# Moving another square of the softmax through DRAM in the attention stage, and queueing the loads behind its return

## The chip, the cores and the metric

The kernel runs on one core of a Trainium2 chip, as one launch. The metric is the device time of one execution in microseconds (us). TensorE is called PE here, VectorE DVE, ScalarE ACT, GpSimd POOL, and SyncE SP. SP computes nothing: it issues the DMAs of this kernel, nearly all of them, in one queue and in the order of the program. POOL issues the scattered row writes.

## The reference

Two layers follow each other. First comes attention with a mask from hashing: a query and a key meet only where the signs of six random projections agree. Then every token goes to the one expert (of 8) that a gate picks.

```python
q_bits = (np.einsum('bhsd,dk->bhsk', q, proj) > 0)      # B=4, H=8, S=768, D=64; proj is 64 x 6
q_bucket = np.sum(q_bits * powers, axis=-1)             # k_bucket likewise
mask = q_bucket[:, :, :, None] == k_bucket[:, :, None, :]
scores = np.where(mask, scale * np.matmul(q, k.transpose(0, 1, 3, 2)), -1000000000.0)
attn = np.exp(scores - np.max(scores, axis=-1, keepdims=True))
attn = attn / (np.sum(attn, axis=-1, keepdims=True) + 1e-09)
out = np.matmul(attn, v)
...
x = out.transpose(0, 2, 1, 3).reshape(B * S, H * D)     # 3072 tokens of 512
expert_idx = np.argmax(x @ w_gate, axis=1)
h = np.maximum(xe @ w1[e], 0.0); out[mask] = gate_w[mask, None] * (h @ w2[e])
```

## The kernel before, in words

**Tiling.** The 32 heads are worked on as 16 pairs, 0 to 15. A pair has two groups, g = 0 and 1, of 384 queries each. A group has six steps, n = 0 to 5, for three blocks of 128 queries (jj) and the two heads of the pair (hh), n = 2·jj + hh. So n = 0 is (jj 0, hh 0), and n = 1 is (jj 0, hh 1), the second step of the group. Each step handles a block of 128 queries by 768 keys. This is the stage that the change touches; it takes the first 480 us or so. The experts' stage behind it is not touched.

**One step.** For step i the program writes, in this order:

- "S", lines L232 and L233: the scores of step i + 2, four matmuls into the PSUM tile `s` (two buffers). The first of each two takes the high part of keys (`k1`), the second the low part together with the twelve rows of hash codes (`k2`, `q2`).
- DVE takes the row maximum of `s` (L235, `m`) and two tiny operations on it (L236, L237).
- ACT takes the exponential of step i + 1 from `s` to the SBUF tile `p`, with the row sums to `sums` (L247). This frees the buffer of `s`.
- "T", L272: six transposes of `p` on PE against the identity into two PSUM tiles `t`, which ACT copies to `pt` (L275, two copies).
- In steps 1, 3 and 5, "AV", L288: eight matmuls of the group before, `pt` with `v`, into `o`. In step 1 "X" follows (L316): three transposes of the result of the group before that one, which DVE multiplies by the reciprocal of the sums (`inv`) into `xr`.

**The moved block.** In one step of a group the six transposes are left out. There the exponential writes its result to `pd` in another order, and the block goes out to a DRAM buffer (`moved`, four DMAs, L257) and back to SBUF (`pq`, one DMA, L260), which moves its 32 by 32 squares to their places. DVE then transposes each square (L263, STREAM_TRANSPOSE) into `pt`. Before the change this is step 0 of 27 groups, all but the first and the last four. DVE works in three parts of 128x256, at the tops of steps 0, 2 and 4 of the next group.

**Loads and operands.** `load_head` (L147 `kr`, L148 `qr`, 384 KB each) is issued a pair ahead of use, `load_codes` (L126, eight DMAs of 192 KB) for two pairs at a time, `load_v` (L153) at step 0 of g = 1. From `qr` POOL makes `q1` (L162, L171), and two DMAs fill `q2` from it and from the codes (L167, L168, in `sent`). From `kr` DVE and POOL make `k1` and `k2` (L178, L179), and one DMA brings the codes' rows into `k2` (L182, named k<-cr). `half_codes` makes the codes (L135 to L137). The list `later` holds DMAs to be issued at the top of a coming step, `heavy` operand work that is popped in steps 1, 3 and 5. In steps 19 to 47 every fourth step issues a `prefill` (L114, xs<-zrow, 910 KB), which writes the rows of the experts' input buffer; that is from pair 1 to the end of pair 3.

**Order.** PE, DVE, ACT and SP run in the written order. POOL's order is chosen by the framework's scheduler when the program is built. A wait of SP holds everything queued behind it.

Of the kernel before, what the change touches and what calls it, by code (L numbers as in the profile page):

```python
# [13 lines left out]
ALU = mybir.AluOpType  # L14
# [4 lines left out]
P = 128  # L19
B, H, S, D = 4, 8, 768, 64  # L20
NB = S // P
NPAIR = H // 2
# [7 lines left out]
SQ = 32  # L30
# [22 lines left out]
def bf(ap):  # L53
    return ap.bitcast(F32)
# [3 lines left out]
def lsh_attention_moe_kernel(ctx, tc, qd, kd, q2d, k2d, v, pjbd, wg, w1, w2, ident_in, tri_in, cols_in, eoff_in, ids_in, out):  # L58
    nc = tc.nc
    V, A, G, PE, SY = nc.vector, nc.scalar, nc.gpsimd, nc.tensor, nc.sync  # L60
# [58 lines left out]
    def load_codes(qi, hf, ks=(0, 1)):  # L119
        if qi not in xqs:  # L120
            xqs[qi] = ({}, codep.tile([P, S], F32R, name="cr"))
        for k in ks:
            pr = 2 * qi + k
            for j, src in enumerate((qd, kd)):
                t = xqp.tile([P, 384], F32, name="xq")
                SY.dma_start(out=t, in_=src[2 * pr:2 * pr + 2].rearrange("h d s -> (h d) s")[:, hf * 384:hf * 384 + 384])  # L126
                xqs[qi][0][(hf, 2 * k + j)] = t
# [13 lines left out]
    operands = {}  # L141

    def load_head(pr, hh):
        h = 2 * pr + hh
        qr = rawp.tile([P, S], F32, name="qr")
        kr = rawp.tile([P, S], F32, name="kr")
        SY.dma_start(out=kr, in_=k2d[h])  # L147
        SY.dma_start(out=qr, in_=q2d[h])  # L148
        return [qr, kr]
# [6 lines left out]
    later = []  # L156

    def q_operands(pr, hh, i):
        qr = operands[pr][0][hh][0]
        q1 = opp.tile([P, S], F32R, name="q1")  # L160
        q2 = opp.tile([P, S], F32R, name="q2")
        G.tensor_copy(out=q1, in_=qr)  # L162
        cr, cbase = codes[pr]
        c0 = cbase + NCODE * hh

        def sent():
            SY.dma_start(out=bf(q2[0:D]), in_=bf(q1[0:D]))  # L167
            SY.dma_start(out=bf(q2[D:D + NCODE]), in_=bf(cr[c0:c0 + NCODE]))  # L168

        later.append((i + 2, sent))  # L170
        G.tensor_tensor(out=q1[D:P], in0=qr[D:P], in1=bf(q1[D:P]), op=ALU.subtract)  # L171
        operands[pr][0][hh] += [q1, q2]

# [66 lines left out]
    def expo(s, m, sums, idx, moves):  # L240
        if moves:
            p = pdp.tile([P, S], F32, name="pd")
            to, of = p.rearrange("p (a c i) -> p c a i", a=4, i=SQ), s[:, 0:S].rearrange("p (c a i) -> p c a i", a=4, i=SQ)
        else:
            p = pp.tile([P, S], F32, name="p")
            to, of = p, s[:, 0:S]
        A.activation(to, of, AF.Exp, bias=m[:, 2:3], scale=m[:, 1:2], accum_out=sums[:, idx:idx + 1])  # L247
        return p

    def move(p, pt):  # L250
        way = moved[next(writes) % 2]
        q = pdp.tile([P, 4, 6, SQ], F32, name="pq")
        to = way.rearrange("(a j) s k -> s j a k", a=4)

        def out():
            for x in range(4):
                SY.dma_start(out=to[x], in_=p[SQ * x:SQ * x + SQ].rearrange("j (a k) -> j a k", a=4))  # L257

        def back():
            SY.dma_start(out=q, in_=way.rearrange("p s (c i) -> p s c i", i=SQ))  # L260

        def turn(c):
            V.transpose(out=pt[:, c:c + 2, 0:P].rearrange("p c (s j) -> p c s j", j=SQ), in_=q[:, :, c:c + 2].rearrange("p s c i -> p c s i"))  # L263

        return out, back, turn

# [13 lines left out]
    ots = {}  # L280
    invs = {}
    late = []

    def av(pr, g, pts, kcs, o, qs=slice(0, 384), heads=(0, 1)):
        vt = operands[pr][1]
        for kc in kcs:
            for hh in heads:
                PE.matmul(out=o[hh * D:hh * D + D, qs], lhsT=vt[:, kc, hh * D:hh * D + D], rhs=pts[hh][:, kc, qs],  # L288
                          start=kc == 0, stop=kc == NB - 1)

    def av_evac(pr, g, sums, o, defer):
        b, pi = divmod(pr, NPAIR)
        ot = otp.tile([P, 384], F32, name="ot")
        if defer:
            late.append(lambda: A.copy(out=ot, in_=o[:, 0:384]))
        else:
            V.tensor_copy(out=ot, in_=o[:, 0:384])
        ots[(b, g, pi)] = ot
        if (b, g) not in invs:
            invs[(b, g)] = smp.tile([P, 3, H], F32, name="inv", bufs=4)  # L300
        inv = invs[(b, g)][:, :, 2 * pi:2 * pi + 2]
        V.tensor_scalar(out=sums, in0=sums, scalar1=1e-9, scalar2=None, op0=ALU.add)
        V.reciprocal(out=inv, in_=sums.rearrange("p (j h) -> p j h", h=2))

    def av_out(pr, g):
        b, pi = divmod(pr, NPAIR)
        ot = ots[(b, g, pi)]
        inv = invs[(b, g)][:, :, 2 * pi:2 * pi + 2]
        if (b, g) not in xrows:
            xrows[(b, g)] = xrp.tile([P, 3, NG, RSEG], F32, name="xr")  # L310
            b0 = b * NB + 3 * g
            V.tensor_copy(out=xrows[(b, g)][:, :, :, SEG].bitcast(I32), in_=ids[:, b0:b0 + 3])
        x = xrows[(b, g)]
        xp = ps_m.tile([P, 512], F32, name="misc")
        for jj in range(3):
            PE.transpose(out=xp[:, jj * P:jj * P + P], in_=ot[:, jj * P:jj * P + P], identity=ident)  # L316
        V.tensor_tensor(
            out=x[:, :, pi, 0:SEG].rearrange("p j (h d) -> p j h d", h=2),
            in0=xp[:, 0:384].rearrange("p (j h d) -> p j h d", j=3, h=2),
            in1=inv.unsqueeze(3).broadcast_to([P, 3, 2, D]),  # L320
            op=ALU.mult)
# [186 lines left out]
    NPR = B * NPAIR  # L508
# [27 lines left out]
    turns = []  # L536

    def group(pr, g):
        if (pr, g) not in grp:
            grp[(pr, g)] = ([ptp.tile([P, NB, 384], F32, name=f"pt{x}", bufs=2) for x in range(2)],  # L540
                            smp.tile([P, 6], F32, name="sums", bufs=4))
        return grp[(pr, g)]

    def run_expo(i):
        pr, g, jj, hh = steps[i]
        moves = jj == 0 and hh == 0 and 0 < 2 * pr + g < 2 * NPR - 4
        p = expo(*soft.pop(i), group(pr, g)[1], 2 * jj + hh, moves)
        if moves:
            out, back, turn = move(p, group(pr, g)[0][hh])
            later.extend([(i, out), (i + 2, back)])  # L550
            turns.extend((i + 6 + c, partial(turn, c)) for c in (0, 2, 4))
        else:
            probs[i] = p

# [16 lines left out]
    def pick_first():  # L571

        def most():
            keys()
            V.reduce_max(out=best[:, 0:1], in_=key, axis=AX.X)

        def which():
            V.tensor_scalar(out=mark[:, 0], in0=key, scalar1=best[:, 0:1], scalar2=None, op0=ALU.is_equal)
            V.tensor_tensor(out=mark[:, 1], in0=mark[:, 0], in1=eoff[:, 0], op=ALU.mult)
            V.reduce_sum(out=best[:, 1:2], in_=mark[:, 1], axis=AX.X)  # L580
            V.tensor_scalar(out=best_i, in0=best[:, 1:2], scalar1=-1.0, scalar2=float(E), op0=ALU.mult, op1=ALU.add)

        return [most, which]
# [115 lines left out]
    light = []  # L699

    def out_and_route(pr, g):
        if pr % NPAIR < NPAIR - 1:
            av_out(pr, g)
            return

        pieces = route(pr // NPAIR, g)
        pieces[0]()
        light.append(lambda: av_out(pr, g))
        light.extend(pieces[1:])
        if (pr, g) == (NPR - NPAIR - 1, 1):  # L710
            light.extend(pick_first())
# [6 lines left out]
    run_scores(1)  # L718
    first_codes = [first_k(1, G), first_q(1, 0)]
    run_expo(0)  # L720
    for f in first_codes:
        f()
    SY.dma_start(out=h0[0][:, 384:S], in_=q2d[0][:, 384:S])
    prev, due, extra = None, [], {}
    for i, (pr, g, jj, hh) in enumerate(steps):
        n = 2 * jj + hh
# [6 lines left out]
            operands[pr + 1][1] = load_v(pr + 1)  # L733
        if pr == 0 and i == 0:
            operands[1] = [[load_head(1, hh) for hh in range(2)], None]
        if g == 1 and n == 1 and pr + 2 < NPR:
            operands[pr + 2] = [[load_head(pr + 2, 0)], None]
        if g == 1 and n == 4 and pr + 2 < NPR:
            operands[pr + 2][0].append(load_head(pr + 2, 1))
        if pr + 4 < NPR and ((pr, g, n) == (1, 0, 0) or g == 1 and n == 2 and pr % 2 == 0 and pr):  # L740
            for x in range(2):
                load_codes((pr + 4) // 2, x)
        if g == 0 and n == 0 and pr + 1 < NPR:
            for x in range(2):
                fs = [partial(q_operands, pr + 1, x), partial(k_operands, pr + 1, x)]
# [27 lines left out]
        if i + 1 < len(steps):  # L773
            run_expo(i + 1)
        while late:
            late.pop(0)()
        pts, sums = group(pr, g)
# [363 lines left out]
    with tc.If(nc.values_load(spare[0:1, E:E + 1], min_val=0, max_val=max(most), skip_runtime_bounds_check_because=why) > 0):  # L1141
# [10 lines left out]
        for e in range(E):  # L1152
            rows_apart("xs", G.indirect_dma_start(out=xs, out_offset=bass.IndirectOffsetOnAxis(ap=row[:, e:e + 1], axis=0),
                                                  in_=pad.rearrange("p g w -> p (g w)"), in_offset=None))
# [62 lines left out]
```

## Time and profile before

| | us |
|---|---|
| three runs before | 765.5, 769.04, 768.43; median 768.43 |
| the profiled execution | 765.38, with a span of 763.5 on the core |
| granted TensorE clock, mean over the span | 0.991 |
| PE busy | 734.3 (96% of the span) |
| DVE, ACT, POOL busy | 531.4 (70%), 459.6 (60%), 334.0 (44%) |
| DMA | 134.23 MB, 176 GB/s over the span |

How to read it: the span starts with the first instruction of the core and ends with the last, and all positions below are microseconds from its start. PE's weight loads are a row of their own (PEld), since they run beside matmuls. Matmuls overlap, so the start of one to the start of the next says more than its duration. A bracket behind a row of the timeline is the idle time of the engine ahead of it, and what the profile takes for the end of that wait. A row with x6 holds six instructions.

### The profile page before, as it was taken

How to read it: one execution, taken by the hardware profiler on the slowest of the kernel's cores; microseconds unless marked ns; L12 is line 12 of the kernel's file. 1: busy time of each engine (PE TensorE's matmuls, PEld its weight loads, DVE VectorE, ACT ScalarE, POOL GpSimd, SP SyncE). 2: the span in 40 equal slices, each digit the busy share in tenths (PEclk: the TensorE clock that was granted, in tenths of full speed). 3: DMA queues.
4: the chain of work that ended last, by engine and by line, in shares of the span. 5: the costliest groups of instructions: out<-in, count | busy, mean ns of one | idle time of the engine just before them, and what ended most of it. 6: DMA issues, size and time to landing. Idle time of an engine off the chain costs nothing.

```text
span 763.5 us, 13596 instructions
## 1 busy us (share of the span) xinstructions
PE 734.3 (96%) x4557; PEld 572.5 (75%) x4557; DVE 531.4 (70%) x1259; ACT 459.6 (60%) x939; POOL 334.0 (44%) x284
## 2 busy tenths in 40 slices
PE   6988997899999999999999999999999999999997
PEld 3645664566666666666667766999999999999995
DVE  6856776588877888877888786765656574665751
ACT  6756776577787777787778885343334343353430
POOL 2743333334632435524343460303747466383572
PEclk9999999799999999999999999999999999999999
DMA  5867798575675485575466330466464646656531
GB/s 180 255 203 227 190 306 242 166 258 146 194 252 172 102 280 159 167 264 161 115 210 203 107 100 29 144 174 171 146 171 143 182 149 190 180 184 192 169 107 45
DMA packets 84047, 134.23 MB, mean 176 GB/s; under 512 B 10278, under 2 KB 52390, under 8 KB 83968
## 3 DMA queue, kind: packets, MB, share of 16 engines
q1 hardware_dynamic: 78976, 120.59, 54.0%
q0 software_dynamic: 4992, 12.69, 4.6%
q8 instruction: 38, 0.62, 0.4%
q14 instruction: 41, 0.34, 0.2%
HBM read 94.37 MB, written 30.98 MB: 164 GB/s over the span
## 4 chain that ended last, share of the span: by engine, by line
PE 47%; issue 21%; POOL 14%; DMA 8%; DVE 6%; SPq 2%; ACT 2%; POOLq 0%; DVEq 0%; ACTq 0%
PE o L288 14%; PE t L272 11%; POOL y L992 10%; PE s L232 9%; PE s L233 7%; DMA y<-yo,tags 3%; DVE m L235 2%; PE misc L316 2%; POOL yo L990 1%; DMA q<-cr 1%; ACT p L247 1%; PE misc L135 1%; DMA qr<-q2d 1%; DMA xr<-xs 1%; DMA xre<-xs 1%
## 5 line engine op out<-in xcount | busy, mean ns | idle before, releaser
L235 DVE TENSOR_REDUCE m<-s 128x1 f32<-128x768 f32 x192 | 181.8, 947 | 54.5 <-PE s L233 43.7
L247 ACT ACTIVATE p<-s,m 128x768 f32<-128x768 f32 x165 | 164.9, 1000 | 61.8 <-DVE m L237 56.0
L275 ACT COPY pt<-t 128x384 f32<-128x384 f32 x330 | 141.1, 481 | 44.5 <-PE t L272 44.4
L232 PE MATMUL s<-k,q 128*128 128x512 f32 (+1 forms) x384 | 149.0, 389 | 5.4 <-ACT p L247 4.8
L288 PE MATMUL o<-pt,vt 128*64 128x384 f32 (+1 forms) x816 | 147.3, 486 | 0.0
L233 PE MATMUL s<-k,q 76*128 76x512 f32 (+1 forms) x384 | 124.7, 345 | 13.3 <-POOL q L171 6.3
L272 PE MATMUL t<-ident,p 128*128 128x128 f32 x990 | 136.9, 274 | 0.0
L232 PEld LDWEIGHTS s<-k,q 128*128 128x128 f32 x384 | 73.5, 191 | 65.4 <-ACT pt L275 22.9
L992 POOL DMA_INDIRECT y<-yo,tags x89 | 104.3, 1172 | 25.2 <-issue 22.5
L272 PEld LDWEIGHTS t<-ident,p 128*128 128x128 f32 x990 | 113.8, 141 | 1.8 <-issue 0.6
L179 POOL TENSOR_TENSOR k<-kr,k 64x768 fp32r<-64x768 f32 x30 | 54.7, 1824 | 125.2 <-DVE k L178 58.8
L233 PEld LDWEIGHTS s<-k,q 76*128 76x128 f32 x384 | 74.0, 193 | 23.8 <-POOL q L171 10.6
L288 PEld LDWEIGHTS o<-pt,vt 128*64 128x64 f32 x816 | 49.6, 137 | 50.7 <-issue 47.8
L950 ACT ACTIVATE hh<-hps 128x352 fp32r<-128x352 f32 (+3 forms) x56 | 27.9, 499 | 97.1 <-PE hps L964 97.1
L657 DVE TENSOR_TENSOR wlo<-wraw,whi 128x1024 fp32r<-128x1024 f32 x60 | 73.7, 1229 | 16.8 <-ACT whi L652 16.8
L983 PE MATMUL hps<-hh,whi 128*128 128x448 f32 (+10 forms) x224 | 76.2, 340 | 0.0
L983 PE MATMUL hps<-hh,wlo 128*128 128x436 f32 (+6 forms) x224 | 76.1, 340 | 0.0
L983 PE MATMUL hps<-hl,whi 128*128 128x436 f32 (+6 forms) x224 | 76.1, 340 | 0.0
L964 PE MATMUL hps<-xh,whi 128*128 128x352 f32 (+3 forms) x224 | 75.0, 335 | 0.0
L964 PE MATMUL hps<-xh,wlo 128*128 128x428 f32 (+6 forms) x224 | 74.8, 334 | 0.0
L964 PE MATMUL hps<-xl,whi 128*128 128x428 f32 (+6 forms) x224 | 74.8, 334 | 0.0
L171 POOL TENSOR_TENSOR q<-qr,q 64x768 fp32r<-64x768 f32 x30 | 55.2, 1841 | 20.4 <-DMA xs<-xr,slot 13.5
(218 smaller groups left out, 1074.8 us busy)
## 6 DMA issues: line engine op xcount, KB each, us to landing
wraw<-w SPq DMA_DIRECT2D x64, 512.0 KB
kr<-k2d SPq DMA_DIRECT2D x32, 384.0 KB
qr<-q2d SPq DMA_DIRECT2D x31, 384.0 KB
moved<-pd SPq DMA_DIRECT2D x108, 96.0 KB
pq<-moved SPq DMA_DIRECT2D x27, 384.0 KB
xs<-zrow SPq DMA_DIRECT2D x8, 910.0 KB
vt<-v SPq DMA_DIRECT2D x16, 384.0 KB
xq<-qd SPq DMA_DIRECT2D x30, 192.0 KB
```

Source lines behind the costliest of these rows:

```text
L171: G.tensor_tensor(out=q1[D:P], in0=qr[D:P], in1=bf(q1[D:P]), op=ALU.subtract)
L232: PE.matmul(out=s[:, c0:c1], lhsT=q1[:, qs], rhs=k1[:, c0:c1], start=True, stop=False)
L233: PE.matmul(out=s[:, c0:c1], lhsT=q2[0:KM, qs], rhs=k2[0:KM, c0:c1], start=False, stop=True)
L235: V.reduce_max(out=m[:, 0:1], in_=s[:, 0:S], axis=AX.X)
L247: A.activation(to, of, AF.Exp, bias=m[:, 2:3], scale=m[:, 1:2], accum_out=sums[:, idx:idx + 1])
L272: PE.transpose(out=t[:, i * P:i * P + P], in_=p[:, kc * P:kc * P + P], identity=ident)
L275: A.copy(out=dst, in_=src)
L288: PE.matmul(out=o[hh * D:hh * D + D, qs], lhsT=vt[:, kc, hh * D:hh * D + D], rhs=pts[hh][:, kc, qs], start=kc == 0, stop=kc == NB - 1)
L657: loeng.tensor_tensor(out=lo[:, i:i + step], in0=cell["t"], in1=bf(hi[:, i:i + step]), op=ALU.subtract)
L964: PE.matmul(out=hps[:, 0:w], lhsT=wt[:, c, fs], rhs=xt[:, c, 0:w], start=n == 0, stop=n == 3 * NDC - 1)
L983: PE.matmul(out=yps[:, 0:w], lhsT=wt[:, f, ds], rhs=ht[:, 0:w], start=n == 0, stop=n == 3 * NFC - 1)
L992: rows_apart("out", G.indirect_dma_start(out=out_seg, out_offset=bass.IndirectOffsetOnAxis(ap=tags[:, i, 0:1].bitcast(I32), axis=0), in_=y ...
```

## The change

It consists of these parts:

- The moved block is that of step 1 of a group (hh = 1), and only in the pairs 4 to 13, which makes 20 groups instead of 27. It goes out at the top of its step and its return is issued two steps later, as before. DVE turns its squares in one operation of 128x768 five steps later, at the top of step 0 of the next group.
- `load_head` of both heads moves from steps 1 and 4 of g = 1 to steps 3 and 4. `load_codes` moves from step 2 of g = 1 of an even pair, where all eight DMAs stood together, to steps 3 and 4 of g = 0, four in each. In the program they then stand behind the return of a block.
- The two DMAs of `sent` are issued one step after the operation instead of two for pair 1.
- The addition of 1e-9 to the sums goes from DVE to POOL for 29 of the groups, and DVE's reciprocal of them is held back until `out_and_route`, two steps later.

```diff
-        later.append((i + 2, sent))
+        later.append((i + (1 if pr == 1 else 2), sent))
...
-        def turn(c):
-            V.transpose(out=pt[:, c:c + 2, 0:P].rearrange("p c (s j) -> p c s j", j=SQ), in_=q[:, :, c:c + 2].rearrange("p s c i -> p c s i"))
+        def turn():
+            V.transpose(out=pt[:, :, 0:P].rearrange("p c (s j) -> p c s j", j=SQ), in_=q.rearrange("p s c i -> p c s i"))
...
-        V.tensor_scalar(out=sums, in0=sums, scalar1=1e-9, scalar2=None, op0=ALU.add)
-        V.reciprocal(out=inv, in_=sums.rearrange("p (j h) -> p j h", h=2))
+        if defer:
+            G.tensor_scalar(out=sums, in0=sums, scalar1=1e-9, scalar2=None, op0=ALU.add)
+            divide.append(lambda: V.reciprocal(out=inv, in_=sums.rearrange("p (j h) -> p j h", h=2)))
+        else:
+            V.tensor_scalar(out=sums, in0=sums, scalar1=1e-9, scalar2=None, op0=ALU.add)
+            V.reciprocal(out=inv, in_=sums.rearrange("p (j h) -> p j h", h=2))
...
-        moves = jj == 0 and hh == 0 and 0 < 2 * pr + g < 2 * NPR - 4
+        moves = jj == 0 and hh == 1 and NPAIR <= pr < NPR - 2
...
-            turns.extend((i + 6 + c, partial(turn, c)) for c in (0, 2, 4))
+            turns.append((i + 5, turn))
...
     def out_and_route(pr, g):
+        while divide:
+            divide.pop(0)()
...
-        if g == 1 and n == 1 and pr + 2 < NPR:
-            operands[pr + 2] = [[load_head(pr + 2, 0)], None]
-        if g == 1 and n == 4 and pr + 2 < NPR:
-            operands[pr + 2][0].append(load_head(pr + 2, 1))
-        if pr + 4 < NPR and ((pr, g, n) == (1, 0, 0) or g == 1 and n == 2 and pr % 2 == 0 and pr):
+        if g == 1 and n in (3, 4) and pr + 2 < NPR:
+            if n == 3:
+                operands[pr + 2] = [[], None]
+            operands[pr + 2][0].append(load_head(pr + 2, n - 3))
+        if (pr, g, n) == (1, 0, 0):
             for x in range(2):
-                load_codes((pr + 4) // 2, x)
+                load_codes(2, x)
+        if pr and pr % 2 == 0 and g == 0 and n in (3, 4) and pr + 4 < NPR:
+            load_codes((pr + 4) // 2, n - 3)
```

On SP, group 1 of pair 3, from its vt load to the first block of pair 4. Numbers at a name tell buffers apart; k<-cr brings key codes. Before:

```order
L153 DMA vt<-v 128x768
L167 DMA q_1485<-q_1484 64x768
L168 DMA q_1485<-cr 12x768
L147 DMA kr<-k2d 128x768
L148 DMA qr<-q2d 128x768
L114 DMA xs<-zrow 112x8x260
L260 DMA pq<-moved_61 128x768
L182 DMA k_1546<-cr 12x768
L147 DMA kr<-k2d 128x768
L148 DMA qr<-q2d 128x768
L114 DMA xs<-zrow 112x8x260
L257 DMA moved_62<-pd 32x4x192 x4
```

The same place now:

```order
L153 DMA vt<-v 128x768
L167 DMA q_1492<-q_1491 64x768
L168 DMA q_1492<-cr 12x768
L114 DMA xs<-zrow 112x8x260
L182 DMA k_1555<-cr 12x768
L147 DMA kr<-k2d 128x768
L148 DMA qr<-q2d 128x768
L147 DMA kr<-k2d 128x768
L148 DMA qr<-q2d 128x768
L114 DMA xs<-zrow 112x8x260
L257 DMA moved_61<-pd 32x4x192 x4
```

The loads of kr and qr and the return of a block, which stood ahead of the key codes, now stand behind them or are gone; the prefill still stands ahead.

On PE, steps 0 and 1 of group 1 of pair 6, from the scores of step 2 on. Before:

```order
L232 MATMUL s<-k_2195,q_2136 128x256
L233 MATMUL s<-k_2196,q_2137 128x256
L232 MATMUL s<-k_2336,q_2274 128x512
L233 MATMUL s<-k_2337,q_2275 128x512
L232 MATMUL s<-k_2336,q_2274 128x256
L233 MATMUL s<-k_2337,q_2275 128x256
L272 MATMUL t<-ident,p 128x128 x6
L288 MATMUL o<-pt_2438,vt 64x384
L288 MATMUL o<-pt_2439,vt 64x384
```

The same place now:

```order
L232 MATMUL s<-k_2199,q_2141 128x256
L233 MATMUL s<-k_2200,q_2142 128x256
L272 MATMUL t<-ident,p 128x128 x6
L232 MATMUL s<-k_2335,q_2275 128x512
L233 MATMUL s<-k_2336,q_2276 128x512
L232 MATMUL s<-k_2335,q_2275 128x256
L233 MATMUL s<-k_2336,q_2276 128x256
L289 MATMUL o<-pt_2439,vt 64x384
L289 MATMUL o<-pt_2440,vt 64x384
```

The six transposes have gone from between the second scores and AV to between the two scores.

On DVE, the end of group 0 and the start of group 1 of pair 6. Before:

```order
L237 TENSOR_SCALAR m<-m 128x1
L302 TENSOR_SCALAR sums<-sums 128x6
L303 RECIPROCAL inv<-sums 128x3x2
L178 CAST k_2628<-kr 128x768
L263 STREAM_TRANSPOSE pt_2438<-pq 128x2x128
L235 TENSOR_REDUCE m<-s 128x1
```

The same place now:

```order
L237 TENSOR_SCALAR m<-m 128x1
L178 CAST k_2642<-kr 128x768
L263 STREAM_TRANSPOSE pt_2440<-pq 128x6x128
L235 TENSOR_REDUCE m<-s 128x1
L236 TENSOR_SCALAR m<-m 128x1
```

The addition to the sums and the reciprocal have left this place, and the turn is the whole block instead of a third of it.

More of the change, by code (lines that the diff above doesn't have):

```diff
@@ L282, in lsh_attention_moe_kernel @@
     late = []
+    divide = []
     def av(pr, g, pts, kcs, o, qs=slice(0, 384), heads=(0, 1)):
```

## The prediction

> **What bounds the kernel now.** I began with the head of the page.
>
> ```profile
> span 763.5 us, 13596 instructions
> PE 734.3 (96%) x4557; PEld 572.5 (75%) x4557; DVE 531.4 (70%) x1259; ACT 459.6 (60%) x939; POOL 334.0 (44%) x284
> ```
>
> PE is the bound, idle for 763.5 − 734.3 = 29 us in all. PE's waits from 30 to 145 us say where it stands still:
>
> ```profile
> PE s L233 <- POOL q L171: 6.3, 1, 6.3
> PE s L233 <- DMA q<-cr: 3.7, 1, 3.7
> PE s L233 <- issue: 2.9, 1, 2.9
> ```
>
> They are single waits, all at the scores of step 1 of a group 0 (pairs 1, 2 and 4). They stand in these stretches, each one step long, with a step of the same work in pair 14 as the fourth row and a step 0 without AV as the fifth (length; PE, PEld, DVE, ACT, POOL busy; granted clock; DMA share; GB/s):
>
> ```profile
> 37.87:47.20 9.33, 5.63 (x29) 2.59 (x27) 2.93 (x8) 4.31 (x9) 6.13 (x5) 0.82 0.86 267
> 71.72:77.82 6.10, 3.21 (x22) 1.76 (x20) 2.84 (x8) 3.19 (x7) 4.22 (x5) 1.00 1.06 356
> 129.02:140.95 11.93, 5.64 (x21) 2.94 (x19) 3.41 (x9) 3.84 (x8) 6.04 (x5) 0.60 0.96 318
> 415.08:418.06 2.98, 2.98 (x22) 1.78 (x20) 2.80 (x9) 2.61 (x7) 0.44 (x1) 1.00 0.98 385
> 418.06:419.45 1.39, 1.39 (x12) 1.29 (x11) 0.40 (x2) 1.39 (x5) 0.00 (x0) 1.00 0.24 54
> 46.42 0.85 PE L135 MATMUL misc<-xq,pj 128*32 128x384 f32 x8
> ```
>
> The first stretch also holds code matmuls (the last row, 46.42 to 47.20, 0.78). The losses are 9.33 − 2.98 − 0.78 = 5.6, 6.10 − 2.98 = 3.1 and 11.93 − 2.98 = 8.9 us: **17.6 us** together. The waits are only 12.9 of them; the rest is the clock, 0.82 and 0.60 there. The timeline of the third:
>
> ```profile
> 125.05 0.46 SPq L147 DMA_DIRECT2D kr<-k2d  x1
> 125.56 0.43 SPq L148 DMA_DIRECT2D qr<-q2d  x1
> 126.04 0.42 SPq L114 DMA_DIRECT2D xs<-zrow  x1
> 126.58 0.49 SPq L260 DMA_DIRECT2D pq<-moved  x1
> 127.11 1.53 SPq L182 DMA_DIRECT2D k<-cr  x1
> 133.61 1.80 POOL L171 TENSOR_TENSOR q<-qr,q 64x768 fp32r<-64x768 f32 x1
> 135.79 0.76 PE L233 MATMUL s<-k,q 76*128 76x512 f32 x1 [6.29 <-POOL q L171]
> ```
>
> The waiting matmul needs the key codes (k<-cr, 36 KB), and they were queued behind 768 KB of heads, 910 KB of prefill and 384 KB of a returning block. The POOL operation named is for the next pair and isn't an operand. In the second stretch the profile names no releaser, in the first a code DMA. I take the code DMA for all three.
>
> **Stalls: what the change removes.** Seven blocks of the pairs 0 to 3 no longer travel (384 KB each way), and heads stand behind the codes. On SP the codes then follow only small copies and, for the second and third stall, one prefill. SP also no longer waits there for a block's landing before its return. For the first stall, `sent` of pair 1 is a step earlier and ahead of the heads. What remains: 910 KB at the 318 GB/s of the third stretch is 2.9 us. A bound for issue to use of a DMA is in these rows, a block's return and its first use, without a wait:
>
> ```profile
> 197.25 3.28 SPq L257 DMA_DIRECT2D moved<-pd  x4
> 202.13 0.34 SPq L260 DMA_DIRECT2D pq<-moved  x1
> 206.55 0.44 DVE L263 STREAM_TRANSPOSE pt<-pq 128x256 f32<-128x256 f32 x1
> ```
>
> That is at most 4.4 us. So codes issued behind a prefill are there after 7.3 us at worst. They are issued for step 2 and read by the scores issued at step 5, 5.8 us later if SP went no faster than PE (steps 2, 3 and 4: 1.39 + 2.98 + 1.39). But nothing in that stretch of SP's queue waits for PE except the load of v, so SP runs ahead. I take the whole gain, **−17.6**; its lower bound is two remainders of 7.3 − 5.8 = 1.5 us, −14.6.
>
> The Trainium skill ("TensorE: Matmul & The Clock Gate", section on the HAM clock gate) says the array falls to half rate after an idle window of about 3.4 us. By that rule remainders of 1.5 us would cost no clock; the trace agrees, since the waits of 6.3 and 3.7 us lowered the clock and that of 2.9 us (granted 1.00) did not.
>
> **Unmoved groups.** Two whole groups, one with a moved block (pair 6, g = 1) and one without (pair 14, g = 0):
>
> ```profile
> 206.69:219.74 13.05, 13.02 (x84) 8.90 (x82) 10.30 (x26) 10.53 (x25) 4.76 (x4) 1.00 0.63 193
> 413.69:427.09 13.40, 13.40 (x90) 9.50 (x88) 10.61 (x30) 11.37 (x27) 5.30 (x4) 1.00 0.45 155
> ```
>
> A moved block saves only 13.40 − 13.05 = 0.35 us today. The seven groups that no longer move pay it back: 7 × 0.35 = 2.5 at least, and where step 0 had saved more (0.81 us long instead of 1.01, as in the first two rows below; so in two of the seven), up to 1.39 − 0.81 = 0.58 each. I take **+3.0**. Their 14 more copies on ACT lie beside PE (ACT 11.37 of 13.40).
>
> **Moved groups.** Why is the saving small? Six transposes cost PE 0.69 us (their weight loads, third row). Before, step 0 without them runs into a full pair of score buffers: the next scores start 212.07 − 211.06 = 1.01 us on, though an unmoved step 0 takes 1.39 with 0.69 of it transposes.
>
> ```profile
> 169.94 0.50 PE L232 MATMUL s<-k,q 128*128 128x512 f32 x1
> 170.75 0.40 PE L232 MATMUL s<-k,q 128*128 128x512 f32 x1
> 203.02 0.69 PEld L272 LDWEIGHTS t<-ident,p 128*128 128x128 f32 x6
> 211.06 0.51 PE L232 MATMUL s<-k,q 128*128 128x512 f32 x1
> 212.07 0.50 PE L232 MATMUL s<-k,q 128*128 128x512 f32 x1
> 213.63 1.51 PE L288 MATMUL o<-pt,vt 128*64 128x384 f32 x8
> 215.38 0.48 PE L232 MATMUL s<-k,q 128*128 128x512 f32 x1
> 213.66 0.99 ACT L247 ACTIVATE p<-s,m 128x768 f32<-128x768 f32 x1 [1.27 <-DVE m L237]
> ```
>
> In step 1, AV and X follow the scores, 215.38 − 213.63 = 1.75 us of work that needs no buffer of `s`. Step 0 then takes 1.39 and step 1 (215.38 − 212.07 = 3.31) falls to 2.62, so the next scores come at 211.06 + 1.39 + 2.62 = 215.07. The exponential that frees their buffer ended at 214.65. So the 0.69 are saved whole: 13.40 − 0.69 = 12.71 per group, 0.34 less than now, × 20 = 6.8. In four of the groups step 0 took 0.81, as in the first two rows, so 0.1 is left there (0.4); for five with routing work beside step 0 I halve it (0.85); eleven gain all (3.7): **−5.0**, between 0 (PE waits for the exponential after all) and −6.8.
>
> **DVE, POOL, SP beside it.** The operations on `sums` (duration least/median/most, ns), then step 0 of pair 6, g = 1, two shapes of a transpose, and two sums of waits:
>
> ```profile
> L302 DVE TENSOR_SCALAR sums<-sums x31: 160/161/1116, 44.2 to 468.9; 128x6 f32<-128x6 f32 x31
> L420 POOL TENSOR_SCALAR sums<-sums x3: 210/216/233, 460.4 to 476.6; 128x2 f32<-128x2 f32 x3
> 210.45 0.16 DVE L302 TENSOR_SCALAR sums<-sums 128x6 f32<-128x6 f32 x1
> 210.64 0.19 DVE L303 RECIPROCAL inv<-sums 128x6 f32<-128x6 f32 x1
> 212.15 0.96 DVE L235 TENSOR_REDUCE m<-s 128x1 f32<-128x768 f32 x1 [0.51 <-PE s L233]
> L598 DVE STREAM_TRANSPOSE xt<-xr 128x448 f32<-128x448 f32 x8 | 4.6, 611 | 0.0
> L598 DVE STREAM_TRANSPOSE xt<-xrl 128x160 f32<-128x160 f32 x4 | 1.3, 335 | 1.8 <-DMA xrl<-xs 1.8
> POOL q L162 <- DMA qr<-q2d: 28.2, 8, 7.6
> DVE pt L263 <- DMA pq<-moved: 2.8, 2, 1.6
> ```
>
> From 160 to 448 elements a transpose grows by 276 ns, so 768 take about 611 + 320 × 0.958 = 0.92 us, against 0.44 for the part that stood there. The two operations on the sums go from this place (0.3), and DVE idled 0.51 us here, so the turn adds nothing to the maximum that follows. If that cover were gone, the cost would be at most 0.48 per group. AV, which reads the turned block, starts after about 2.1 us, the turn ends near 1.2. POOL gains 29 small additions; its nearest row is 128x2 at 216 ns, and POOL is 44% busy. The reciprocal waits for one two steps later (1.39 + 2.98 = 4.4 us), longer than two of POOL's operations of 1.80 (L171). If POOL stood in a wait for qr just then, DVE would wait with it, up to 7.6 − 4.4 = 3.2 us; that belongs to the first rival.
>
> The Trainium skill ("SBUF — State Buffer", section on the two sides of SBUF) speaks against this: VectorE and GpSimd share a port pair that one holds alone for a whole instruction. At 216 ns each, 29 more holds are 6.3 us, on the sum 0, because DVE has slack in every group; the trace has the lock's mark, L302 which lasts 0.16 us in most cases and 1.1 at worst.
>
> **The sum.** 765.38 − 17.6 + 3.0 − 5.0 = 745.8, against the profiled execution (span 763.5 and 1.9 around it). The median shown is 3.05 higher than that execution. I expect less spread without stalls and add 1.2, a part of it: **747**.
>
> **Rivals.**
> 1. *A wait for DMA stays in the early pairs* (prefill ahead of codes, or a load of heads now too late for POOL's cast, which already waited up to 7.6 us for qr). Half of the 17.6 remains: 747 + 8.8 = 756. For it: 910 KB still stand ahead, DMA share near 1. Against it: 7 × 768 KB less traffic there.
> 2. *Step 1 saves nothing*, because the exponential (0.4 us early by the sum above) comes late with the longer turn. Then a moved group takes 13.05 as now: 747 + 5.0 = 752.
> 3. *Slower: the return comes too late for the turn.* The block leaves one step later and is turned at the same step 0, three steps after its return's issue instead of four. In the order now: out 1.0 us after the scores of step 0, return 4.9 later (202.13 − 197.25), landed at most 4.4 later, so at 10.3, turn at 12.6: 2.3 us to spare. Each us beyond holds DVE, then AV, in 20 groups; the gain of 19.6 in the sum is gone at 0.98 us of mean wait. With 1.5 us: 746 + 30 = 776. For it: DVE already waited for a return twice, 2.8 us in all. Against it: loads now stand behind the return, and the DMA share in these groups is 0.63.
> 4. *No change that can be told*: stalls come back at other places of the early pairs, costing all 17.6, and the moved groups gain as much as the unmoved ones lose: 765.
>
> **How the numbers follow.** The forecast 0.68, rival 1 0.14, rival 2 0.10, rival 3 0.04, rival 4 0.04. The range takes rivals 1 and 2 in above (756) and below the whole −6.8, +2.5 and some relief for the first groups, which I put at 2 to 3 us: 741. Within 0.5% (3.8 us), about what a measurement of this kernel can tell from no change, lies rival 4; beyond it on the slow side rival 3. So faster 0.92, same 0.04, slower 0.04.
>
> **What would show it.** PE's waits at L233 in the pairs 1, 2 and 4 gone, clock 1.00 throughout those groups; group lengths near 12.7 us in the pairs 6 and 7 and 13.4 in the unmoved ones; step 0 at 1.39 and step 1 at 2.62; L263 twenty times at 0.92 us, with no wait for pq. A wait of DVE for pq, or of the reciprocal for POOL, would make it wrong.

## The result, and the profile after

The changed kernel takes 744.31 us (median of 4 runs, 743.5 to 745.42), and the kernel before took 767.97 beside it on the same chip (4 runs). The ratio is 0.9697, with a 95% interval of 0.967 to 0.9724: faster by 3%. The forecast was 747, with a range of 741 to 756. The profiled execution took 744.31 itself, with a span of 742.4. Some numbers of lines shift by a few: AV is L289 now, the sums are added on POOL at L304 and the reciprocal is L305. All ratios leave out the slow executions: one of 1426.59 us in experiment 2, one of 766.42 in experiment 5 and one of 785.68 of the kernel before, beside the experiments 10 to 12.

The head of the page after:

```profile
span 742.4 us, 13583 instructions
PE 728.5 (98%) x4599; PEld 575.5 (78%) x4599; DVE 516.6 (70%) x1169; ACT 466.2 (63%) x953; POOL 341.3 (46%) x313
```

PE is idle for 13.9 us instead of 29. Its waits in the attention stage (from 12 to 450 us) are almost gone; the three of 6.3, 3.7 and 2.9 us have become one of 0.5:

```profile
PE s L232 <- ACT p L247: 1.9, 4, 0.7
PE s L233 <- DMA k<-cr: 0.5, 1, 0.5
```

Where the 765.38 − 744.31 = 21.1 us went is seen from three stretches that begin and end at the same instructions: the groups 0 to 8 (numbered over all pairs, so that 8 is g = 0 of pair 4), the groups 9 to 27, and the rest. Columns are length; PE, PEld, DVE, ACT, POOL busy; granted clock; DMA share; GB/s. Before:

```profile
6.81:150.82 144.01, 127.58 (x762) 82.20 (x763) 99.57 (x239) 97.70 (x210) 56.39 (x40) 0.95 0.76 226
150.82:413.69 262.87, 260.92 (x1696) 174.46 (x1695) 216.00 (x599) 203.45 (x449) 111.84 (x82) 1.00 0.63 188
413.69:763.50 349.81, 343.39 (x2097) 315.41 (x2095) 212.87 (x418) 155.76 (x279) 164.56 (x157) 1.00 0.49 146
```

After:

```profile
7.22:135.46 128.24, 126.05 (x805) 85.20 (x805) 90.81 (x210) 102.59 (x223) 58.24 (x48) 1.00 0.69 208
135.46:392.36 256.90, 256.90 (x1696) 174.34 (x1694) 210.50 (x543) 204.99 (x449) 116.73 (x101) 1.00 0.65 192
392.36:742.40 350.04, 342.86 (x2097) 315.52 (x2095) 212.03 (x411) 155.64 (x278) 165.17 (x159) 1.00 0.50 147
```

The early groups gave 15.8 us, although PE has 43 more matmul records there; the groups 9 to 27 gave 6.0 with the same number of matmuls. In them PE is now busy without a gap (256.90 of 256.90). The rest (the last four groups and the experts' stage) is as it was, and the start is 0.4 later.

The three stretches that held the stalls, then a group with a moved block (pair 10, g = 0) and one without (pair 14, g = 0), after:

```profile
37.89:42.42 4.53, 3.99 (x29) 1.92 (x28) 2.34 (x6) 3.85 (x9) 2.20 (x3) 1.00 0.88 305
67.80:70.79 2.99, 2.99 (x21) 1.77 (x19) 2.33 (x6) 2.60 (x7) 2.89 (x3) 1.00 0.89 275
122.94:125.94 3.00, 3.00 (x22) 1.79 (x20) 2.33 (x6) 2.61 (x7) 2.91 (x3) 1.00 0.93 321
285.75:298.50 12.75, 12.75 (x85) 8.89 (x81) 10.55 (x23) 10.62 (x24) 8.70 (x8) 1.00 0.78 237
392.36:405.76 13.40, 13.40 (x89) 9.51 (x87) 10.35 (x25) 11.32 (x26) 5.54 (x5) 1.00 0.54 179
```

The steps of 9.33, 6.10 and 11.93 us are 4.53, 2.99 and 3.00, all at a granted clock of 1.00. An undisturbed first one would be 2.98 + 0.78 = 3.76, so 0.77 us are left there, and nothing in the other two. The 0.5 us wait in it ends at 38.91, 0.14 after the key codes land (38.77); SP's issue just ahead of theirs, `sent`'s q<-cr, took 1.99 us in this execution. SP at the third of these places, after:

```profile
113.72 0.50 SPq L114 DMA_DIRECT2D xs<-zrow  x1
114.27 0.74 SPq L182 DMA_DIRECT2D k<-cr  x1
119.74 0.33 SPq L147 DMA_DIRECT2D kr<-k2d  x1
```

The scores that read these codes (L233) start at 123.26 without a wait (the timeline of PE), 9.0 us after the issue. By its semaphore events in the trace the DMA landed at 120.30, after 6.0 us; that of pair 2 took 6.6. Before, PE went on 8.7 us after the issue (127.11 to 135.79), and the same events settle what it waited for in all three places: the key codes landed at 74.99 and 135.70 and PE went on at 75.08 and 135.79; at the first place the queries' codes of `sent` (q<-cr) landed at 41.91 and PE went on at 42.05.

Steps 0 and 1 of group 0 of pair 10, on PE, DVE and ACT, after (three pieces of the timeline):

```profile
290.13 0.50 PE L232 MATMUL s<-k,q 128*128 128x512 f32 x1
291.52 0.48 PE L232 MATMUL s<-k,q 128*128 128x512 f32 x1
292.39 1.51 PE L289 MATMUL o<-pt,vt 128*64 128x384 f32 x8
294.14 0.48 PE L232 MATMUL s<-k,q 128*128 128x512 f32 x1
...
289.52 0.97 DVE L263 STREAM_TRANSPOSE pt<-pq 128x768 f32<-128x768 f32 x1
291.22 0.96 DVE L235 TENSOR_REDUCE m<-s 128x1 f32<-128x768 f32 x1 [0.73 <-ACT pd L247]
...
292.71 0.99 ACT L247 ACTIVATE p<-s,m 128x768 f32<-128x768 f32 x1 [0.37 <-DVE m L237]
```

Step 0 takes 1.39, step 1 2.62. The exponential that frees the buffer ends at 293.70, 0.44 before it is needed. The turn ends 1.9 before AV reads it, and the maximum behind it waits for ACT, not for the turn. The groups of the new operations (busy, mean ns | idle before):

```profile
L263 DVE STREAM_TRANSPOSE pt<-pq 128x768 f32<-128x768 f32 x20 | 19.4, 969 | 0.0
L304 POOL TENSOR_SCALAR sums<-sums 128x6 f32<-128x6 f32 x29 | 6.9, 237 | 39.4 <-ACT p L247 30.3 <-DMA pq<-moved 7.6
L305 DVE RECIPROCAL inv<-sums 128x6 f32<-128x6 f32 x29 | 5.2, 181 | 0.0
```

DVE waited for a returned block in no group, and for POOL's sums in none.

### The profile page after: what moved, and what is told of

It reads as the page before. It is cut to its first block, busy times and chain, and to the rows that moved or that the text cites. A ratio compares the mean times of both kernels' runs of the same rounds, so it can differ in the third digit from the quotient of the medians.

```text
span 742.4 us, 13583 instructions
## 1 busy us (share of the span) xinstructions
PE 728.5 (98%) x4599; PEld 575.5 (78%) x4599; DVE 516.6 (70%) x1169; ACT 466.2 (63%) x953; POOL 341.3 (46%) x313
## 4 chain that ended last, share of the span: by engine, by line
PE 56%; issue 20%; POOL 13%; DMA 6%; SPq 2%; DVE 1%; ACT 1%; POOLq 0%; DVEq 0%; ACTq 0%
PE o L289 17%; PE t L272 14%; POOL y L1001 11%; PE s L232 11%; PE s L233 9%; DMA y<-yo,tags 2%; PE misc L321 2%; PE misc L135 1%; POOL yo L999 1%; DMA xr<-xs 1%; DMA xre<-xs 1%; PE misc L343 1%; DMA qr<-q2d 1%; PE s L693 1%; DMA xq<-qd 0%
## 5 line engine op out<-in xcount | busy, mean ns | idle before, releaser
L235 DVE TENSOR_REDUCE m<-s 128x1 f32<-128x768 f32 x192 | 183.2, 954 | 54.9 <-PE s L233 28.8
L247 ACT ACTIVATE p<-s,m 128x768 f32<-128x768 f32 x172 | 171.4, 997 | 49.7 <-DVE m L237 35.5
L275 ACT COPY pt<-t 128x384 f32<-128x384 f32 x344 | 147.1, 481 | 38.7 <-PE t L272 38.5
L289 PE MATMUL o<-pt,vt 128*64 128x384 f32 (+1 forms) x816 | 144.9, 479 | 0.0
L272 PE MATMUL t<-ident,p 128*128 128x128 f32 x1032 | 141.6, 273 | 0.0
L233 PE MATMUL s<-k,q 76*128 76x512 f32 (+1 forms) x384 | 124.2, 344 | 0.5 <-DMA k<-cr 0.5
L272 PEld LDWEIGHTS t<-ident,p 128*128 128x128 f32 x1032 | 118.0, 141 | 1.5 <-ACT p L247 0.6
L289 PEld LDWEIGHTS o<-pt,vt 128*64 128x64 f32 x816 | 49.1, 136 | 48.8 <-issue 45.6
L233 PEld LDWEIGHTS s<-k,q 76*128 76x128 f32 x384 | 74.2, 193 | 9.8 <-POOL cr L137 0.8
L960 DVE SCALAR_TENSOR_TENSOR hl<-hps,hh 128x352 fp32r<-128x352 f32 (+3 forms) x56 | 31.7, 565 | 45.2 <-ACT hh L959 44.7
```

Of the source, the lines that this page charges most:

```text
L233: PE.matmul(out=s[:, c0:c1], lhsT=q2[0:KM, qs], rhs=k2[0:KM, c0:c1], start=False, stop=True)
L235: V.reduce_max(out=m[:, 0:1], in_=s[:, 0:S], axis=AX.X)
L272: PE.transpose(out=t[:, i * P:i * P + P], in_=p[:, kc * P:kc * P + P], identity=ident)
L275: A.copy(out=dst, in_=src)
```

## The experiments

They ran in four sets, each set on one chip beside the kernel before; ratios are to that. Its medians were 767.95 (experiments 1 to 4), 776.65 (5, 7, 8, 9), 772.36 (10 to 12) and 766.18 (13), and what follows group 27 (the last four groups and the experts' stage), of which the edits touch group 28 alone and only in 10 and 13, took 350 to 362 us in the profiles. So the lengths of two stretches in the profiled executions tell more than the totals. The groups 0 and 1 took 28.8 to 32.7 us, by the clock and with no order in it by the edits (see the last section), and are left out. "Early steps" are the three that held the stalls (undisturbed 3.76, 2.99, 2.99).

| kernel | groups 2 to 8 | groups 9 to 27 | early steps | ratio (95%) |
|---|---|---|---|---|
| before | 114.34 | 262.87 | 9.33, 6.10, 11.93 | 1 |
| 1 before, blocks only in pairs 4 to 13 | 105.47 | 264.37 | 9.67, 3.93, 3.00 | 0.9844 (0.9789–0.9899) |
| 2 before, new places of the loads | 101.18 | 263.28 | 5.42, 4.34, 3.92 | 0.983 (0.9761–0.9899) |
| 3 after, block in step 0 | 98.54 | 262.84 | 3.76, 2.99, 2.99 | 0.9787 (0.9731–0.9843) |
| after | 98.97 | 256.90 | 4.53, 2.99, 3.00 | 0.9697 (0.967–0.9724) |
| after, once more | 98.22 | 257.55 | 3.78, 2.99, 3.00 | 0.9664 (0.9606–0.9721) |
| 8 after, no block moved | 98.94 | 270.60 | 3.85, 2.99, 2.99 | 0.9883 (0.9831–0.9934) |
| 13 after, 25 groups | 95.71 | 257.17 | 3.87, 2.99, 2.99 | 0.9675 (0.9648–0.9702) |

**1. Only the early blocks away** (in the kernel before):

```diff
-        moves = jj == 0 and hh == 0 and 0 < 2 * pr + g < 2 * NPR - 4
+        moves = jj == 0 and hh == 0 and NPAIR <= pr < NPR - 2
```

> The kernel before, with the moved blocks (still step 0, turned in three parts) cut to the pairs 4 to 13 and nothing else changed. Theory A (the stalls come from everything queued ahead of the codes: returning blocks, heads and prefill together): the blocks are gone from the early pairs, heads and prefill still stand ahead, so about half of the 17.6 us of stalls stay and seven unmoved groups cost 1 to 3 us: 757 to 762 us. Rival B (the blocks' traffic and SP's waits for it are the whole cause): no stall stays, 768 - 17.6 + 2 = 752 us. Rival C (the place of the loads is the whole cause): the stalls stay, 768 to 770 us.

The time is 755.53 us, under theory A's range and over rival B's 752. It isn't half of each stall that stays: the third is gone, the second falls to 0.9 us and the first stays whole. Its wait, and the steps:

```profile
PE s L233 <- POOL q L162: 2.9, 1, 2.9
```
```profile
37.94:47.61 9.67, 6.76 (x29) 3.14 (x27) 2.82 (x8) 4.31 (x9) 6.50 (x5) 0.65 0.58 181
72.98:76.91 3.93, 3.21 (x21) 1.76 (x20) 2.61 (x8) 3.18 (x7) 1.57 (x2) 1.00 0.98 317
129.20:132.20 3.00, 3.00 (x22) 1.79 (x20) 2.60 (x8) 2.69 (x7) 2.15 (x3) 1.00 1.02 347
```

So the first stall isn't made by blocks. The profile puts its wait down to POOL's L162, but the last operand to land before PE goes on (41.33) is `sent`'s q<-q, at 41.08; 768 KB of heads stood ahead of it in SP's order.

**2. Only the new places of the loads** (in the kernel before):

```diff
-        if g == 1 and n == 1 and pr + 2 < NPR:
-            operands[pr + 2] = [[load_head(pr + 2, 0)], None]
-        if g == 1 and n == 4 and pr + 2 < NPR:
...
+        if g == 1 and n in (3, 4) and pr + 2 < NPR:
...
+        if pr and pr % 2 == 0 and g == 0 and n in (3, 4) and pr + 4 < NPR:
+            load_codes((pr + 4) // 2, n - 3)
```

> The kernel before, with only the places of the loads of heads and codes changed as in the change; the 27 blocks stay at step 0. Theory A: SP still waits for blocks in the early pairs and their traffic stays, so about half of the stalls go: 757 to 762 us. Rival B (blocks are the whole cause): no change, 768 us. Rival C (loads are the whole cause): all stalls go, 768 - 17.6 = 750 us.

```profile
37.84:43.26 5.42, 4.00 (x30) 1.92 (x27) 3.17 (x8) 3.97 (x9) 2.30 (x3) 1.00 0.97 323
67.78:72.12 4.34, 3.22 (x22) 1.77 (x20) 2.84 (x9) 3.19 (x7) 0.80 (x1) 1.00 0.93 290
124.16:128.08 3.92, 3.21 (x21) 1.76 (x19) 2.83 (x9) 3.19 (x7) 0.80 (x1) 1.00 0.93 282
```

754.02 us, again under theory A's range; neither rival's extreme came. All three stalls shrink, to remainders of 1.7, 1.3 and 0.9 us, and the clock stays at 1.00. What is left of the first ends as `sent`'s q<-cr lands (39.64, PE at 39.73); a returning block stood ahead of it in SP's order. A new 1.1 us appears in step 1 of group 6, where DVE waits 2.7 us for the block of group 5. So the two parts overlap: the cut alone takes 8.9 us off the groups 2 to 8 and the loads alone 13.2, but both together (experiment 3, which also has the earlier `sent` and the sums on POOL) 15.8, since the third stall, 8.9 us in itself, goes nearly whole by either. Neither alone does it.

**3. The changed kernel with its block in step 0:**

```diff
-        moves = jj == 0 and hh == 1 and NPAIR <= pr < NPR - 2
+        moves = jj == 0 and hh == 0 and NPAIR <= pr < NPR - 2
...
-            turns.append((i + 5, turn))
+            turns.append((i + 6, turn))
```

> The changed kernel with the moved block put back at step 0 of the 20 groups and turned in one operation six steps later; all else as changed. If the gain in the moved groups comes from the step (AV fills the wait for the buffer of scores), plain groups go back from 12.7 to 13.05 us and the time rises by 5 to 6 us to 749 to 750. Rival (the gain there comes from the one turn and the lighter DVE): no change, 744 to 745 us.

```profile
136.99:399.83 262.84, 261.00 (x1697) 174.67 (x1695) 207.44 (x543) 203.43 (x449) 116.72 (x101) 1.00 0.63 186
290.14:303.24 13.10, 13.03 (x85) 8.91 (x81) 10.45 (x23) 10.45 (x24) 8.66 (x8) 1.00 0.72 224
```

The groups 9 to 27 are back at 262.84 (before: 262.87), and the same group of pair 10 at 13.10 instead of 12.75. The median is 751.31 us, 7.0 above the change's where 5 to 6 were expected, but the stretch gives back 5.9. So the 5.9 us of these groups come from the step that the block is taken from, and not from the rest of the change, which is in place here too.

**8. No block moved** (the changed kernel, `moves = False`):

> The changed kernel without any moved block; all transposes are on PE. If each moved block at step 1 saves the whole 0.69 us of six transposes, 20 groups give it back: 744.3 + 13.7 = 758 us, with plain groups of 13.4 us. If the saving were only as large as that of step 0 before (0.35), 751 us.

```profile
293.34:306.73 13.39, 13.39 (x91) 9.50 (x88) 9.60 (x22) 11.26 (x26) 8.71 (x8) 1.00 0.82 260
135.17:405.77 270.60, 268.86 (x1811) 185.94 (x1809) 196.94 (x522) 218.89 (x486) 117.44 (x102) 1.00 0.40 127
```

A moved block in step 1 is worth (270.60 − 256.90) / 19 = 0.72 us a group, in step 0 only (270.60 − 262.87) / 19 = 0.41. Six transposes cost 0.69: in step 1 they are saved whole. The stretch with 19 of the groups is 13.7 us longer, where 13.7 was expected of all 20. The early steps are free of stalls here too.

**4. All 27 groups, in step 1** (the changed kernel with the old condition on groups, `0 < 2 * pr + g < 2 * NPR - 4`):

> The changed kernel with blocks moved (step 1) in the early pairs too, 27 groups as before the change. Each of the seven groups more can save 0.69 us, 4.8 us in all. Theory A: the blocks come back into the crowded early pairs, part of the stalls returns and takes the 4.8 away or more: 744 to 752 us. Rival B (blocks are the whole cause): the stalls return, 744 - 4.8 + 17 = 756 us. Rival C (loads are the whole cause): no stall, 739.5 us.

It takes 746.91 us, ratio 0.9739 (0.9686 to 0.9792). The early groups do get shorter (two plain ones of pair 2 take 12.74 instead of 13.40), but step 1 of group 6 takes 7.17 us instead of 3.28, because the block of group 5 came back late. The total lies in theory A's range. PE's wait, the waits of DVE for blocks, and that step:

```profile
PE o L289 <- DVE pt L263: 2.8, 1, 2.8
```
```profile
DVE pt L263 <- DMA pq<-moved: 6.4, 3, 5.4
```
```profile
96.29:103.46 7.17, 4.41 (x18) 1.97 (x17) 3.52 (x8) 1.94 (x6) 0.18 (x1) 0.86 0.97 305
```

This is the third rival's mechanism (the return too late for the turn), at the place where experiment 2 had it too.

**10. Six more groups** (2, 3, 4, 5, 7 and 28):

```diff
-        moves = jj == 0 and hh == 1 and NPAIR <= pr < NPR - 2
+        moves = jj == 0 and hh == 1 and (2 <= 2 * pr + g <= 5 or 7 <= 2 * pr + g < 2 * NPR - 3)
```

> The changed kernel with six groups more that move their block (step 1): both groups of the pairs 1 and 2, group 1 of pair 3, and group 0 of pair 14; not group 1 of pair 0 nor group 0 of pair 3, where the run with 27 groups showed the codes late and the turn 2.8 us late. Each saved 0.63 to 0.69 us there: 6 x 0.65 = 3.9 us less than the changed kernel beside it, 0.965 of the time before, if no new wait comes. Rival (blocks in the early pairs delay codes or each other even so): the gain shrinks to 0 to 2 us.

750.8 us, ratio 0.97 (0.965 to 0.9751), against 746.36 of the changed kernel on the same chip: no gain, as the rival had it. The six were shorter by 0.63 to 0.69 each, 3.9 us in all, but group 5's block was late again and made group 6 2.9 us longer (the start of the profiled execution was also 2.2 us slower, see the last section):

```profile
DVE pt L263 <- DMA pq<-moved: 4.2, 1, 4.2
```
```profile
98.23:104.04 5.81, 4.38 (x24) 2.26 (x22) 3.35 (x8) 1.95 (x6) 0.00 (x0) 1.00 0.93 286
```

**13. The same without group 5** (`2 <= 2 * pr + g <= 4 or 7 <= ...`; groups 2 and 3 are those of pair 1, 4 is g = 0 of pair 2, 7 is g = 1 of pair 3, 28 is g = 0 of pair 14):

> The kernel with the change, with five more groups at step 1 (g = 0 and 1 of pair 1's second, pair 2's first and pair 3's second half, and pair 14's first: groups 2, 3, 4, 7 and 28 of 0 to 31), so 25 in all; group 5, whose block came back late in the run with 26 groups, stays out. If that late return is a matter of group 5's place alone: step 1 of group 6 is back at 3.28 us, the five groups are 0.65 us shorter each, and the time is 3 us under the changed kernel's: a ratio of about 0.963 to the kernel before. If any further block in the early pairs makes some transfer late: another step of the groups 3 to 8 is longer by 1 us or more, and the ratio stays at 0.966 to 0.970.

```profile
37.18:132.89 95.71, 95.71 (x635) 64.72 (x631) 72.38 (x162) 76.41 (x167) 41.29 (x35) 1.00 0.80 248
97.06:100.33 3.27, 3.27 (x24) 2.07 (x23) 2.40 (x7) 2.90 (x8) 0.79 (x1) 1.00 1.01 378
390.06:402.80 12.74, 12.74 (x84) 8.87 (x82) 10.31 (x25) 10.63 (x24) 5.53 (x5) 1.00 0.74 235
```

Step 1 of group 6 (second row) is back at 3.27, and the groups 2 to 8 fall by another 2.5 us, to 95.71 with PE busy throughout. The median, 742.49 us (741.27 to 742.97), is the lowest of all, but the ratio of 0.9675 isn't the expected 0.963 and can't be told from the change's own 0.9697 and 0.9664; the gain of about 3 us is shown by the groups, not by the total.

**5. Each prefill issued twice** (in the changed kernel; the second zeroes further rows of the same buffer):

```diff
+        for r0 in (e * XROWS, e * XROWS + C):
...
+            SY.dma_start(out=halves, in_=zrow...broadcast_to([TB, 2 * NTB, ROW // 2]))
```

> The changed kernel with every prefill issued twice (the second to rows of the same buffer that nothing reads here), so 1.8 MB instead of 0.9 stand ahead of the key codes in the early pairs; the places of heads and blocks as changed. In the changed kernel the codes of the second and third old stall were issued at 59.20 and 114.27 and were needed about 9 us later. Theory A (codes wait for what is queued ahead of them): 2.9 us more ahead, so they come about as late as they are needed; waits of 0 to 1 us at each place, 744.5 to 747 us. Rival B (only blocks and SP's waits for them mattered): no change, 744 to 744.5 us. Rival D (the DMA engines were simply full in the early pairs, whatever stands where): stalls of several us and a lower clock return, 752 us or more.

The ratio of 0.9762 (0.9659 to 0.9865) can't be told from the change's own, but the profile shows a loss. The second stall's step is 3.16, the third's is a stall again, longer than theory A allowed:

```profile
122.19:132.31 10.12, 5.64 (x22) 2.94 (x20) 2.34 (x6) 3.84 (x8) 2.24 (x3) 0.68 0.92 260
```

PE's scores waited until 127.15 there (4.48 us). SP's part of the timeline shows why it is more than the longer transfer:

```profile
112.94 2.14 SPq L167 DMA_DIRECT2D q<-q  x1
...
115.94 2.72 SPq L114 DMA_DIRECT2D xs<-zrow  x2
118.70 2.07 SPq L182 DMA_DIRECT2D k<-cr  x1
```

The codes' transfer took 8.4 us instead of 6.0, and it was issued at 118.70 instead of 114.27, though PE had come to this step 0.75 earlier: several of SP's issues take about 2 us here. So the codes come late by two parts, a transfer 2.3 us longer with more bytes ahead of it and an issue 4.4 us later, which no theory had. A wait of several us with a lower clock is also the sign of rival D, and this run alone doesn't refute it; against D stands experiment 2, where the bytes of the kernel before, in another order, made stalls of 1.7, 1.3 and 0.9 us instead of 5.6, 3.1 and 8.9.

**7. The sums back on DVE:**

```diff
-        if defer:
-            G.tensor_scalar(out=sums, in0=sums, scalar1=1e-9, scalar2=None, op0=ALU.add)
...
+        V.tensor_scalar(out=sums, in0=sums, scalar1=1e-9, scalar2=None, op0=ALU.add)
+        V.reciprocal(out=inv, in_=sums.rearrange("p (j h) -> p j h", h=2))
```

> The changed kernel with the addition to the sums back on DVE and the reciprocal right behind it, as before the change. By the prediction these operations lie in DVE's idle time: no change, within 1 us of 744.3. Rival (DVE is late for the maximum of step 2 when turn and sums stand together): step 1 grows by 0.1 to 0.3 us in some of the 20 groups, 746 to 749 us.

753.25 us, ratio 0.9697 (0.9647 to 0.9747), the change's own. Plain groups stay at 12.75. Groups with routing beside them grow a little (step 1 from 3.09 to 3.29 in groups 9, 17 and 25), as the rival said but in fewer groups; the stretch 9 to 27 is 258.15, longer by 0.6 to 1.2 us than in the two profiles of the changed kernel. This part of the change is worth at most that.

**11. The turn in three parts** (of 128x256, at steps 0, 2 and 4 as before):

```diff
-            turns.append((i + 5, turn))
+            turns.extend((i + 5 + c, partial(turn, c)) for c in (0, 2, 4))
```

> The changed kernel with the turn in three parts (at the tops of steps 0, 2 and 4 of the next group) instead of one operation; the block still leaves in step 1. By the prediction the turn lies in DVE's idle time either way: no change against the changed kernel beside it, within 1 us. Rival (one operation of 0.92 us delays the maximum of step 2): 20 groups gain 0.05 to 0.1 us each, 1 to 2 us less. Rival the other way (three operations cost DVE 0.37 us more a group and later steps wait): 1 to 3 us more.

748.54 us, ratio 0.9685 (0.9621 to 0.975); groups 9 to 27 take 256.80 against 256.90. The single operation brings nothing that can be measured.

**9. `sent` of pair 1 at its old step** (`later.append((i + 2, sent))`):

> The changed kernel with the two DMAs of the queries' operand for pair 1 again two steps after the operation. Theory: the first old stall (pair 1, 5.6 us, 0.8 left after the change) went because of this and because heads no longer stand ahead; the loads do most of it, so 0.5 to 1.5 us come back: 745 to 746 us. Rival (the earlier issue did it alone): the stall is back with its lower clock, 748 to 750 us.

753.72 us, ratio 0.9707 (0.9644 to 0.977). The first stall's step is 3.77, undisturbed; the groups 0 and 1 had been slower there (32.7 us, at a clock of 0.50 for 6.8 us), which gives the codes more time. So this run can't show what the move of `sent` is worth. That it may be worth something is seen in experiment 2, where `sent` is at its old step, the start was at full clock, and the last 1.7 us of the first stall end with its landing.

**12. The changed kernel once more**, beside 10 and 11:

> The changed kernel itself, unaltered, as the measure for the two beside it on the same chip: 0.970 of the time before.

746.36 us, ratio 0.9664 (0.9606 to 0.9721). Its first early step is 3.78, so the 0.77 us left in the first profile are not in every execution; the issue of q<-cr that had taken 1.99 us there took 0.75 here.

## Why the prediction was right

The total came within 0.4%, and each term had its sign; the sizes, against the profiled execution before:

- *Stalls, −17.6.* Measured −16.8 (17.6 less the 0.77 left), in the second profile of the changed kernel the whole. The forecast took a code DMA for the cause of all three without a proof; the landings (41.91, 74.99 and 135.70, PE going on 0.09 to 0.14 later) show that it was right. That the codes came late by what stood ahead of them in SP's order is shown by experiments 1 and 2, which take some of it away or move it behind. For the first, where it is the queries' codes of `sent` and not the key codes, experiment 1 narrows it: it goes by the places of the loads, not by the blocks. The bound of 7.3 us for the codes behind a prefill held: 6.0 and 6.6. That SP runs ahead was right as well (it issued those of pair 4 8.7 us before their scores began at 122.94, not 5.8).
- *The clock.* Remainders of 0.9 to 1.7 us (experiment 2) left it at 1.00, as the forecast said of 1.5. Of the longer waits, 2.9 us cost no clock in the kernel before but lowered it to a mean of 0.65 over the step in experiment 1; 2.8 us lowered it to 0.86 (experiment 4) and 4.48 us to 0.68 (experiment 5). The Trainium skill ("TensorE: Matmul & The Clock Gate", section on the HAM clock gate) says that the window of about 3.4 us is free-running. With the idle window that the prediction quotes from the same page, no wait of 2.9 us would count, since it can't fill one; the runs differ (0.65 and 0.86 after 2.9 and 2.8 us), and they decide: a window that is idle in part can be enough. So the agreement that the prediction saw holds for the kernel before alone.
- *Unmoved groups, +3.0: too large.* Groups 1 to 7 without their stalls cost 1.9 more than before: five of them +0.02, +0.29, +0.35, +0.25 and −0.19, the two with a stall about +0.57 and +0.55. The step that failed is the price of 0.35 to 0.58 for every group: in group 1 PE waited for the exponential anyway (1.37 us before, 0.70 after), so its transposes came free, and group 7 had been disturbed before.
- *Moved groups, −5.0: too small.* The groups 9 to 27 gave 5.97 and group 8 gave 0.36, 6.3 in all, near the lower bound of −6.8. The plain ones came to 12.75 (forecast 12.71) with steps of 1.39 and 2.62, as worked out, with 0.44 us to spare for the exponential. Three of the four whose step 0 took 0.81 (10, 18 and 26) gained 0.1 or nothing, as forecast, the fourth (20) 0.47. What failed is the halving for groups with routing: they gained too, in step 1 (group 16: step 1 from 3.80 to 3.09, the group from 14.20 to 13.90). Experiment 3 shows that the step is the cause, 8 that the transposes are saved whole.
- *DVE and POOL, 0.* Right: 969 ns for the turn (forecast 0.92), no wait for `pq`, none for the sums. Undoing them (7, 11) changed 0 to 1 us. The mark of a lock that the prediction saw in L302 is one in the kernel before: ten of its 31 operations took 0.32 to 1.12 us, and each of the ten ended 0.02 to 0.04 us after an operation of POOL had ended (the longest at 252.31, POOL's L171 at 252.27).
- *The 1.2 us added for the median* weren't there: the profiled execution is the median.

So the mechanisms were right. That the total came within 0.4% is in part luck: the unmoved groups, the moved groups and the median were each put 1.1 to 1.3 us too high, and the 0.8 us too much on the stalls hid part of it.

Of the rivals, the wait that stays in the early pairs is 0.5 us in one profile of the changed kernel and none in the other, and it took a second prefill to bring back a stall (5); step 1 that saves nothing is refuted by 3 and 8. The late return is real, but only where blocks travel in the early pairs (2, 4, 10). No sum of new stalls near 17.6 us came up in any kernel.

## What to carry to other kernels

In this kernel a transfer of 36 KB took 8.6 and 9.1 us behind about 2 MB in its queue, and 6.0 and 6.6 behind 0.9 MB; whether that is a stall was decided by how far ahead of its use SP issued it (8.7 us in the changed kernel). Taking bytes away and moving them behind removed the same third stall, so the two gains didn't add: test each alone. Work taken off the bound engine counted whole only where no buffer limited the next step: take it from the step whose other work needs none, here 0.72 us a group in step 1 against 0.41 in step 0. And before such a step is spread to more places, see whether its round trip meets other traffic: one late block (group 5) ate 2.9 of the 3.9 us that six more had gained.

## What the runs showed that was not expected

- Most issues of a DMA by SP take 0.3 to 0.8 us, but a few take 1.8 to 2.7. Between 30 and 150 us there are 5 of these in the kernel before, 6 in the changed one and 15 in experiment 5, where the codes went out 4.4 us later. That more bytes in flight slow the issuer is the likely reading; no run separates it.
- Groups 0 and 1, which no experiment meant to touch, took 28.8 to 29.7 us in nine profiles and 30.6 to 32.7 in the other five. Those five are the ones in which the granted clock fell there: to 0.50 for 3.4 us from about 15 us on (experiments 3, 11, 13) and for 6.8 us from 14.3 us on (9 and 10). No wait of PE between its first scores and that was longer than 1.2 us; in experiment 9 PE was busy for 1.87 of the 3.41 us before. Why it fell in some executions and not in others is open. The two stretches of experiment 9 (columns as above):

```profile
10.87:14.28 3.41, 1.87 (x10) 1.30 (x10) 3.18 (x9) 2.44 (x5) 1.00 (x2) 1.00 0.69 215
14.28:21.11 6.83, 6.19 (x17) 3.86 (x18) 3.99 (x10) 4.27 (x10) 1.04 (x1) 0.50 0.11 25
```

- Group 5's block alone was late because it left late, not because its return was slow. In experiments 4 and 10 its first DMA went out 6.7 and 6.0 us after PE had begun step 1 of the group; for the groups 2 to 4 and 6 to 8 that was 3.3 us at most. Its return took 5.0 and 4.5 us, where the returns of those groups took 3.3 to 5.4. On SP code loads stood ahead of it, two of the eight of which took 1.7 us to issue. In experiment 4, where PE began the step at 83.53:

```profile
83.58 1.66 SPq L126 DMA_DIRECT2D xq<-kd  x1
90.19 1.88 SPq L257 DMA_DIRECT2D moved<-pd  x4
94.72 0.34 SPq L260 DMA_DIRECT2D pq<-moved  x1
```

Moving those code loads away from the block wasn't tried.
